# New plan values, the first query block ahead in the head, and the last store on ScalarE's queue

## Chip, cores, metric

One NeuronCore of a Trainium2 chip. The metric is the device time of one execution in microseconds (us); lower is better. Compared are medians and ratios of fast runs. What is read here are the 95% intervals in brackets.

## The reference

Two attention branches over the same `x` (2048 tokens, model width 512, 32 heads of width 16) are mixed by a gate:

```python
def _A_ref(x, wqkv, wo):                     # softmax attention
    q, k, v = ...                            # from x @ wqkv, 32 heads of 16
    p = softmax(einsum("bhqd,bhkd->bhqk", q, k) * 16 ** -0.5)
    return (p @ v, heads joined) @ wo
def _B_ref(x, wqkv, w_phi, wo):              # linear attention with a softmax feature map
    phi_q, phi_k = ...                       # [softmax(q w_phi), softmax(-q w_phi)], same for k
    o = phi_q (phi_k^T v) / (phi_q . sum(phi_k) + 1e-6)
    return (o, heads joined) @ wo
g = sigmoid((x * gate_w).sum(-1))
return g * a + (1 - g) * b
```

(Shortened; the data are bfloat16.) The work that counts is the exponential of 32 x 2048 x 2048 scores.

## The kernel before

Scores are made by PE into a ring of PSUM banks (`ps_ring`, line 934), ScalarE takes the exponential of 1024 columns at a time into `ET` (line 952), and PE multiplies `ET` with V (line 991). 95 key tiles of four heads each go another way, so that ScalarE has less to do: DVE turns their scores into integers (`EW`), GpSimd and DVE work out a polynomial from them, and a DMA of 512 KB adds the two parts up in `ED`; PE then multiplies `ED` with V:

```python
hs = [s.op("pool", ..., lambda e, c=c: e.tensor_scalar(                     # L1079, HS pieces
    self.ED[:, ed.idx, W * c:W * c + W].bitcast(dt.int16), half(1, dt.int16, c, W), 128.0, float(EM), ...
u = s.op("dve", 1.13, lambda e: e.tensor_tensor(self.Em[:], Ef(), Ef(), ALU.mult), ...        # L1084
q = s.op("dve", 0.6, lambda e: e.tensor_scalar(self.Em[:], self.Em[:], E3, E1, ...            # L1086
g_ = s.op("dve", 1.13, lambda e: e.tensor_tensor(Ef().bitcast(dt.int16), Ef(), self.Em[:], ALU.mult), ...  # L1088
v = s.op("pool", SWD[0], lambda e: e.dma_start(                             # L1091
    out().bitcast(dt.int16), Ef().bitcast(dt.int16), accum_op=ALU.add), [g_] + hs, ...)
v.kind = "acc"
...
return s.op("pe", 0.2155, ..., fns=[pv(i) for i in range(4)], deps=vs + [...])   # L1102: waits for the DMA
```

PE's gaps are filled with matmuls by zero (line 1010), most of them 64 rows by 512 columns:

```python
lambda e: e.matmul(self.ps_ot[c:c + nc, :], self.iden[r:r + nr, 0:nc], self.zero[r:r + nr, :], ...)
```

The softmax here doesn't subtract the row's maximum and nothing guards it: scores larger than these inputs give would overflow.

## Time and profile before

| | us |
|---|---|
| time, median of 3 (all) | 823.13 (821.17 to 823.39) |
| first exponential, end of the last | 10.27, 813.00 |
| ScalarE's waits in between | 5.0 in nine pieces of 0.17 or more |
| tail after the last exponential | 7.2 |

From the groups of before, the matmuls that use `ED` (in the last column the idle time just ahead of them, and who ended it):

```profile
L1102 PE MATMUL ps_ot<-ED,Vaug 128*17 128x512 bf16 x380 | 37.3, 383 | 3.7 <-DMA ED<-Ef 3.7
L1102 PEld LDWEIGHTS ps_ot<-ED,Vaug 128*17 128x17 bf16 x380 | 9.2, 87 | 25.4 <-issue 18.0 <-DMA ED<-Ef 7.1
```

The median flight of 4.5 us is under the 4.85 that the plan assumes, so in most cases PE comes to a landed `ED`.

### The profile page before, as it was taken

To read this page: it belongs to the slowest core of one execution; us is meant where nothing else is said; L and a number is where in the kernel's file an instruction comes from. 1 tells how busy PE (TensorE), PEld (TensorE's weight loads), DVE (VectorE), ACT (ScalarE), POOL (GpSimd) and SP (SyncE) were. 2 spreads that over 40 slices of the span, in tenths; PEclk is the share of its full clock that TensorE was granted. 3 is DMA by queue.
4 is the path that set the end of the run, shared out by engine and by line. 5 is a ranking of instruction groups with operands and counts; after the bars stand their busy time and mean duration, and the time that the engine had idled before them with its cause. 6 is when DMAs were issued, how large, how long until landed. Compare 5 with 4: busy or idle time off the path is not lost.

```text
span 820.2 us, 15193 instructions
## 1 busy us (share of the span) xinstructions
PE 766.2 (93%) x6063; PEld 231.3 (28%) x6063; DVE 765.7 (93%) x1140; ACT 801.5 (98%) x906; POOL 396.7 (48%) x451
## 2 busy tenths in 40 slices
PE   8998999999999999999999999889899888989998
PEld 3332333232333333222222222222222222222222
DVE  7999989998689999999999999999999999998993
ACT  6999999899999999999999999999999999999997
POOL 2436435432144555565445654554355555654560
PEclk9999999999999999999999999999999999999999
DMA  6455442444326544446445544543544445424433
GB/s 124 115 100 106 82 97 59 96 95 87 61 54 126 108 90 82 100 94 99 99 93 108 117 96 100 108 94 80 105 78 99 92 97 100 88 56 81 81 71 84
DMA packets 96598, 75.85 MB, mean 92 GB/s; under 512 B 76816, under 2 KB 84368, under 8 KB 96528
## 3 DMA queue, kind: packets, MB, share of 16 engines
q0 software_dynamic: 13680, 49.81, 31.0%
q1 hardware_dynamic: 81504, 24.55, 14.5%
q8 instruction: 48, 0.79, 0.4%
q10 hardware_dynamic: 1344, 0.52, 0.3%
q14 instruction: 22, 0.18, 0.1%
HBM read 3.69 MB, written 2.10 MB: 7 GB/s over the span
## 4 chain that ended last, share of the span: by engine, by line
ACT 70%; DVE 15%; PE 9%; DMA 4%; issue 1%; POOL 1%; ACTq 0%; SPq 0%; POOLq 0%
ACT ET L952 67%; DVE EW L1046 5%; DMA ED<-Ef 4%; PE ps_ring L934 3%; DVE Ef L1088 3%; ACT phi L1250 3%; DVE Em L1084 3%; PE ps_mp L775 2%; DVE Ef L1075 1%; DVE Em L1086 1%; PE ps_ot L991 1%; PE ps_mp L1041 1%; PE ps_mp L856 1%; POOL ED L1079 0%; PE ps_ot L1102 0%
## 5 line engine op out<-in xcount | busy, mean ns | idle before, releaser
L952 ACT ACTIVATE ET<-ps_ring 128x1024 bf16<-128x1024 f32 x834 | 775.2, 1215 | 5.1 <-PE ps_ring L934 4.9
L934 PE MATMUL ps_ring<-qT,kT 64*128 64x512 bf16 x1668 | 325.8, 386 | 38.2 <-ACT ET L952 25.0
L1079 POOL TENSOR_SCALAR ED<-EW 128x512 int16<-128x512 int16 (+1 forms) x266 | 234.4, 907 | 211.3 <-DVE Ef L1088 80.2
L1046 DVE TENSOR_SCALAR EW<-ps_mp 128x512 int32<-128x512 f32 (+1 forms) x306 | 238.4, 811 | 15.5 <-PE ps_mp L1041 14.2
L934 PEld LDWEIGHTS ps_ring<-qT,kT 64*128 64x128 bf16 x1668 | 79.9, 93 | 314.0 <-ACT ET L952 299.7
L991 PE MATMUL ps_ot<-ET,Vaug 128*17 128x512 bf16 x1668 | 148.5, 383 | 0.9 <-DVE T L1131 0.8
L1091 POOL DMA_DIRECT2D ED<-Ef x95 | 86.4, 910 | 109.8 <-DVE Ef L1088 52.3
L1084 DVE TENSOR_TENSOR Em<-Ef 128x2048 f16<-128x2048 f16 x95 | 123.0, 1295 | 0.3
L1075 POOL TENSOR_SCALAR Ef<-EW 128x1024 f16<-128x1024 uint16 (+1 forms) x83 | 79.3, 955 | 86.2 <-DVE EW L1046 20.9
L1088 DVE TENSOR_TENSOR Ef<-Ef,Em 128x2048 int16<-128x2048 f16 x95 | 118.6, 1249 | 0.5
L1041 PE MATMUL ps_mp<-qT,kT 64*128 64x512 bf16 (+1 forms) x380 | 108.4, 380 | 3.0 <-DVE EW L1046 1.2
L1010 PE MATMUL ps_ot<-zero,iden 64*128 64x512 bf16 (+2 forms) x502 | 107.9, 377 | 0.0
L1075 DVE TENSOR_SCALAR Ef<-EW 128x1024 f16<-128x1024 uint16 (+1 forms) x129 | 83.4, 657 | 0.2
L1086 DVE TENSOR_SCALAR Em<-Em 128x2048 f16<-128x2048 f16 x95 | 70.3, 740 | 0.1
L991 PEld LDWEIGHTS ps_ot<-ET,Vaug 128*17 128x17 bf16 x1668 | 33.4, 87 | 77.8 <-issue 69.7
L775 PE MATMUL ps_mp<-Wp,xT 128*128 128x512 bf16 x128 | 42.2, 385 | 0.0
L1250 ACT ACTIVATE phi<-ps_mp 128x512 bf16<-128x512 f32 x64 | 39.7, 757 | 1.9 <-PE ps_mp L775 1.9
L1102 PE MATMUL ps_ot<-ED,Vaug 128*17 128x512 bf16 x380 | 37.3, 383 | 3.7 <-DMA ED<-Ef 3.7
L775 PE MATMUL ps_mp<-xT,WA 128*128 128x512 bf16 (+1 forms) x128 | 39.9, 384 | 0.4 <-ACT xT L760 0.3
L1041 PEld LDWEIGHTS ps_mp<-qT,kT 64*128 64x128 bf16 (+1 forms) x380 | 28.4, 94 | 35.3 <-DVE EW L1046 14.4
L1010 PEld LDWEIGHTS ps_ot<-zero,iden 64*128 64x128 bf16 (+2 forms) x502 | 32.0, 94 | 15.6
L1131 DVE STREAM_TRANSPOSE T<-ps_ot 128x512 f32<-128x512 f32 x31 | 22.0, 709 | 3.9 <-PE ps_ot L991 3.5
(93 smaller groups left out, 411.4 us busy)
## 6 DMA issues: line engine op xcount, KB each, us to landing
ED<-Ef POOLq DMA_DIRECT2D x95, 512.0 KB, 4.5
qT<-qst SPq DMA_DIRECT2D x120, 16.0 KB, 2.0
out_dram<-outt SPq DMA_DIRECT2D x12, 128.0 KB, 1.8
WA<-in_A_wqkv_dram SPq DMA_DIRECT2D x3, 384.0 KB, 4.3
phiT<-phi SPq DMA_TRANSPOSE x48, 3.1
WBV<-in_B_wqkv_dram SPq DMA_DIRECT2D x1, 512.0 KB, 6.8
Wp<-in_A_wo_dram SPq DMA_DIRECT2D x1, 512.0 KB, 6.3
WBV<-in_B_wo_dram SPq DMA_DIRECT2D x1, 512.0 KB, 8.5
```

The costliest lines, as they stand in the source:

```text
L775: m = s.op("pe", self.c_mm(n), lambda e, c=c: e.matmul(self.bk(b)[:, 0:n], lhs(c), rhs(c), start=(c == 0), stop=(c == 3)), deps if c == 0 ...
L934: return lambda e: e.matmul(self.ps_ring[:, x % RING, :], self.kT[r, g // 2, kt * P:(kt + 1) * P], self.qT[r, n % 2, i, :], start=True, st ...
L952: self.o_exp.append(s.op("act", w * 0.434 + 0.039, lambda e, b0=b0, s0=s0, w=w: e.activation(self.ET[:, s0:s0 + w, :], self.ps_ring[:, b0: ...
L991: return lambda e: e.matmul(self.ps_ot[32 * i:32 * i + VSL, :], self.Vaug[:, kt, h, :], self.ET[:, (4 * p + k) % NSLOT, :], start=(kt == 0 ...
L1010: return lambda e: e.matmul(self.ps_ot[c:c + nc, :], self.iden[r:r + nr, 0:nc], self.zero[r:r + nr, :], start=False, stop=False, tile_posi ...
L1041: return lambda e: e.matmul(bank(), self.kT[r, cp, kt * P:(kt + 1) * P], self.qT[r, n % 2, i, :], start=True, stop=True, tile_position=(r. ...
L1046: return s.op("dve", dur, lambda e: e.tensor_scalar(self.EW[:, ew.idx, x * QCH:(x + w) * QCH].rearrange("p (b q) -> p b q", b=w) if w > 1 else
L1075: fs = [s.op("pool", U * 8.26e-4 + 0.28, lambda e, c=c: e.tensor_scalar(self.Ef[:, ef.idx, U * c:U * c + U], half(0, dt.uint16, c, U), flo ...
L1079: hs = [s.op("pool", W * 8.26e-4 + 0.165, lambda e, c=c: e.tensor_scalar(self.ED[:, ed.idx, W * c:W * c + W].bitcast(dt.int16), half(1, dt ...
L1084: u = s.op("dve", 1.13, lambda e: e.tensor_tensor(self.Em[:], Ef(), Ef(), ALU.mult), fs + [self.ed_prev], pr, port=True)
L1088: g_ = s.op("dve", 1.13, lambda e: e.tensor_tensor(Ef().bitcast(dt.int16), Ef(), self.Em[:], ALU.mult), [q], pr, port=True)
L1091: v = s.op("pool", SWD[0], lambda e: e.dma_start(out().bitcast(dt.int16), Ef().bitcast(dt.int16), accum_op=ALU.add), [g_] + hs, pr, frees= ...
```

## The change

Its intent: plan values that were searched again, an earlier first exponential, and an earlier last store. The diff, with values cut:

```diff
-PACE = [1.0638464291072671, 0.45790104673263465]
+PACE = [1.0771457571608845, 0.4579007635970128]
-PIECES = ((2, 2), (2, 4), (4, 4))
+PIECES = ((2, 2), (2, 4), (4, 4), (2, 1), (4, 1))
... LEAD, BOUNDS, RULES, AFF, PAIR, JOINT, OFF, PRI, SHY, FILL, SLIP, POLY, SHAPE: new values
-DVE_COUNT = (..., 3, 4, 4, 2, 4, 2, 3, 4, ...)      # blocks 16 to 23
+DVE_COUNT = (..., 3, 3, 4, 3, 4, 3, 2, 4, ...)      # the sum stays 95
@@ emit_qT
-   [o_ev, self.o_par, self.o_qz[n]], 30 * n - 60 + 2 * x, 12 * n, frees=[st], port=True)
+   [o_ev, self.o_par, self.o_qz[n]], (30 * n - 60 + 2 * x) if n or x > 1 else x - 80, 12 * n, frees=[st], port=True)
@@ store
-   self.stores.append(s.op("sp", 0.06, lambda e: e.dma_start(out2d[t * P:(t + 1) * P, :], src()), [dep],
-        prio, dma=P * D * 2, frees=frees))
+   self.stores.append(s.op("act" if t == NT - 1 else "sp", 0.06, lambda e: e.dma_start(out2d[t * P:(t + 1) * P, :], src()), [dep],
+        1e5 if t == NT - 1 else prio, dma=P * D * 2, frees=frees))
```

A piece whose second number is 1, `(2, 1)` or `(4, 1)`, lets GpSimd write all 2048 columns of `ED` in one instruction.

## The prediction

> **What bounds the kernel now.** I read the page's busy shares first, then its costliest groups, then all the waits of ScalarE, then head and tail in order of time.
>
> ```profile
> PE 766.2 (93%) x6063; PEld 231.3 (28%) x6063; DVE 765.7 (93%) x1140; ACT 801.5 (98%) x906; POOL 396.7 (48%) x451
> L952 ACT ACTIVATE ET<-ps_ring 128x1024 bf16<-128x1024 f32 x834 | 775.2, 1215 | 5.1 <-PE ps_ring L934 4.9
> L1250 ACT ACTIVATE phi<-ps_mp 128x512 bf16<-128x512 f32 x64 | 39.7, 757 | 1.9 <-PE ps_mp L775 1.9
> ```
>
> ScalarE (ACT) is the bound: 98% busy, with 834 exponentials of the softmax scores and 64 of the linear branch. PE and DVE at 93% are near, but PE fills its gaps with matmuls by zero. In the chain that ended last, this runs without a break:
>
> ```profile
> 702.89 108.28 ACT ET L952 x118
> ```
>
> 108.28 / 118 = 0.918 us from one exponential to the next (the 1215 ns of one overlap the next). The chain also has two phi activations in 0.98 us at 106.75. So ScalarE's work is 834 x 0.918 + 32 x 0.98 + 0.14 (two gate activations) = 765.6 + 31.4 + 0.1 = 797.1 us. From 10.27 us, the first exponential, to 813.00, the end of the last, there are 802.7 us. The waits of ScalarE in between:
>
> ```profile
> ACT ET L952 <- PE ps_ring L934: 4.9, 9, 1.9
> ACT phi L1250 <- PE ps_mp L775: 1.9, 1, 1.9
> ```
>
> Of the 4.9 us, 1.87 is the wait for the very first exponential. Left are 3.1 + 1.9 = 5.0 us in nine pieces. 797.1 + 5.0 is 802.1, so the account closes to 0.6 us. Only three things can move the end: when the first exponential starts (10.27), those 5.0 us, and the tail of 820.2 - 813.0 = 7.2 us.
>
> [...]
>
> [...] the flight: 1.7 to 1.8 us for all four last stores.
>
> [...] GpSimd's TENSOR_SCALAR into ED takes 607 to 2115 ns over its forms. At 511.01 a 1024-wide one takes 2.10 us beside DVE work, at 514.35 one takes 1.03.
>
> **The change, part by part.** The plan values feed a scheduler that orders the instructions at build time; I compared the two builds' orders.
>
> *Work.* The number of key tiles given to DVE is 95 in both; one moves from query block 17 to 19 and one from 22 to 21. So ScalarE keeps 834 + 64 activations: change 0. On DVE, conversions into EW go from 74 to 92 double-width and from 232 to 196 single: 18 x 1.218 - 36 x 0.681 = -2.6 us. Ef goes from 105 to 95 wide ones and from 24 to 36 narrow: -10 x 0.708 + 12 x 0.434 = -1.9. Together -4.5 us on an engine beside the bound. On GpSimd, ED becomes 86 of 1024, 136 of 512 and 18 new ones of 2048 (before: 114, 152, none). From 701 and 1181 ns I estimate 2.14 us for one of 2048: -28 x 1.181 - 16 x 0.701 + 18 x 2.14 = -5.8; Ef there adds 12 x 0.616 - 2 x 1.063 = +5.3; net about -0.5. None of this is on the path by itself.
>
> *Head.* Before, the order of time shows:
>
> ```profile
> 8.63 0.35 DVE L796 TENSOR_SCALAR qT<-qst,par 128x512 bf16<-128x512 bf16 x1
> 8.90 0.55 DVE L840 CAST kT<-ps_mp 128x384 bf16<-128x384 f32 x1
> 9.37 0.87 DVE L796 TENSOR_SCALAR qT<-qst,par 128x512 bf16<-128x512 bf16 x3
> 9.50 0.23 PEld L775 LDWEIGHTS ps_mp<-WA,xT 128*128 128x128 bf16 x4 [0.49 <-DVE kT L840]
> 10.27 12.02 ACT L952 ACTIVATE ET<-ps_ring 128x1024 bf16<-128x1024 f32 x13 [1.87 <-PE ps_ring L934]
> ```
>
> The first score pair needs two qT pieces. A kT copy sits between them on DVE, and PE stands four V matmuls, which wait for that copy, ahead of the score. In the new order both qT pieces come first and those four matmuls come after the score. The second qT then starts at about 8.90 instead of 9.37: -0.47 us. The first score moves from 9.84 to about 9.3 to 9.4, the first exponential from 10.27 to about 9.8. The second score still needs the last two qT pieces, which end as before, and PE has two key matmuls ahead of it. It ran at 10.29 and its exponential can start at about 10.73, just as the first one's 0.92 us ends. I take -0.45 us, kept as long as nothing later has a fixed time: ScalarE ran from 10.27 to 69.8 without one wait, so there is room.
>
> *Tail.*
>
> ```profile
> 815.79 1.26 ACT L1386 ACTIVATE outz<-ps_mp,gcol 128x512 bf16<-128x512 f32 x2 [2.80 <-PE ps_mp L1345]
> 816.51 1.88 SPq L1353 DMA_DIRECT2D out_dram<-outz  x4
> 816.95 0.69 ACT L1386 ACTIVATE outz<-ps_ring,gcol 128x512 bf16<-128x512 f32 x1
> 817.94 0.45 SPq L1353 DMA_DIRECT2D out_dram<-outz  x1
> ```
>
> The last evacuation ends at 816.95 + 0.69 = 817.64, but its store is issued at 817.94, behind the third, which went at 817.46. An unqueued one follows its activation by 0.04 (816.51 after 816.47). From ScalarE's own queue it can go at about 817.7: -0.25 us. ScalarE's issues in the head took 0.45 us each, as this one on SP did, so the issue costs nothing more. Evacuations and final matmuls are otherwise in the same order.
>
> *The middle.* The 5.0 us are the rest. The long ones are 0.62 and 0.60 at 69.81 and 73.27 (block 2), 1.94 at 148.29 (block 4), 0.32 at 515.62, 0.60 at 550.24 and 0.20 at 580.00 (blocks 19 to 22). In the two of block 2 and those at 515 and 550, PE stood just before in front of a matmul that waits for an ED transfer, for 0.5 to 0.95 us, with the next scores behind it in its order. The new plan touches those places: other priorities and sharing rules in block 2, other pieces in blocks 4 and 5, and the tile counts of blocks 20 to 22 become 4, 3, 2 from 4, 2, 3. A plan that was chosen again probably removes more of these than it makes. I guess that 5.0 becomes about 3.5: -1.5, the softest term.
>
> Sum: -0.45 - 0.25 - 1.5 = -2.2. From the median of 823.13 that is 820.9 us, a ratio of 0.997.
>
> **Rivals.** First: the head start is given back. If the second score waits for key matmuls that PE now stands ahead of it (their inputs are transposes still landing around 9 to 10 us), ScalarE idles after its first exponential and the gain is 0. [...] Against: before, those matmuls at 10.61 waited only for DVE. The time would be about 821.4.
>
> Second: GpSimd becomes the brake. 18 instructions of about 2.1 us [...]; ED then lands late, PE stands in front of it and the score ring runs dry. For: that is how the waits at 69.81, 73.27 and 550.24 arise, and the last block, with four tiles, now has this shape. Against: GpSimd is 48% busy, [...] and PE's waits for ED are only 3.7 + 7.1 us in all. With a fifth of them losing 1 us each it would cost about 4 us: 825.
>
> Third: the new plan removes nearly all waits of the middle: -4.5 instead of -1.5, and 818.
>
> Fourth: the moved store saves nothing, because ScalarE pays for its issue or for the wait on its own last activation: 0.25 us, too little to see in the total.
>
> **Range and chances.** The hard floor is -0.45 - 0.25 - 5.0 = -5.7 us, or 817.4: even removing every wait is 0.7%, so 2% faster (806.7) is out of reach without less ScalarE work. 2% slower (839.6) needs more than 16 us of new waits, three times all there are. The spread of the runs of before is 821.17 to 823.39, so a median can be off by a microsecond. Eight in ten: 818.3 to 823.9. Faster by over 2%: 0.01; within 2%: 0.98; slower by over 2%: 0.01.
>
> **What would show it.** Right: 834 exponentials at 0.918 us in unbroken stretches, the first at 9.7 to 9.9; the last store on ScalarE's queue within 0.1 us of its activation's end; ScalarE's waits between first and last exponential at 2 to 5 us; the tail about 6.9. Wrong in the head: the first exponential early but a wait of 0.4 us or more before the second or third. Wrong in the middle: waits above 6 us with PE in front of ED matmuls, beside GpSimd's 2048-wide instructions. The whole account is wrong if ScalarE's waits do not explain the difference of the spans to within a microsecond.

(For the exponential the sum used the measured 0.918 us. For the store the page of before gives 1.71 to 1.83 us from issue to landing for the last four, all issued from SP; that the move to ScalarE's queue leaves the flight as it is was not shown. The first rival's order on PE is that of the trace of after, shown with the head below.)

## More of the kernel before

The order of all instructions on each engine is made while the kernel is built, by a list scheduler with estimated durations. It takes an `ED` transfer as landed a fixed time after its issue, `CLEAR[3]`:

```python
CLEAR = [3.0, 1.2, 0.97, 4.85, ...]
if o.kind == "acc":
    o.end = max([o.start + (CLEAR[3] + 0.7 if turns and o.start - turns[-1] < 2.4 else CLEAR[3])] + ...)
```

Each engine is given its instructions in that order, with semaphores for what they wait on.

From the page of before, the `ED` row of the DMA issues (number, size, median us from issue to landing) and the queue that carries packets of the kind "instruction" (packets, MB, share of 16 engines):

```profile
q8 instruction: 48, 0.79, 0.4%
...
ED<-Ef POOLq DMA_DIRECT2D x95, 512.0 KB, 4.5
```

## The result and the profile after

| | before | after |
|---|---|---|
| time, median us (range, runs) | 822.43 (821.17 to 823.39, 6) | 825.62 (822.64 to 826.96, 6) |
| ratio to before, 95% interval | | 1.0037, 1.0016 to 1.0057 |
| first exponential, end of the last (profiled run) | 10.27, 813.00 | 9.24, 813.76 |
| ScalarE's waits in between (all gaps) | 5.2 | 6.8 |
| `ED` landings of 5.2 us or more, of 95 | 8 | 19 |
| longest `ED` flight | 6.7 | 7.7 |

Ratios in this text are the mean time of one kernel's fast runs over the mean of the other's fast runs of the same rounds on the same chip, so not quite the ratio of the medians beside them. The changed kernel is slower by 0.37%, where 0.27% faster was predicted. The profiled run (822.64) is the fastest of the six, so its trace understates the loss.

The page of after, busy shares and the costliest group:

```profile
PE 761.8 (93%) x6038; PEld 229.7 (28%) x6038; DVE 760.7 (93%) x1124; ACT 801.7 (98%) x906; POOL 394.8 (48%) x435
L952 ACT ACTIVATE ET<-ps_ring 128x1024 bf16<-128x1024 f32 x834 | 775.5, 1215 | 6.8 <-PE ps_ring L934 6.4
```

ScalarE does the same work at the same pace (834 exponentials, 1215 ns each). What differs is in its waits, here all that lie between its first and last exponential (us, times, longest):

```profile
ACT ET L952 <- PE ps_ring L934: 6.4, 11, 1.8
ACT phi L1250 <- PE ps_mp L775: 1.3, 1, 1.3
ACT ET L952 <- PE ps_mp L1041: 0.3, 1, 0.3
```

(The first of these also holds 1.3 us before the very first exponential, which do not belong to them.) **The head**, in order of time, after:

```profile
8.81 0.39 PE L934 MATMUL ps_ring<-qT,kT 64*128 64x512 bf16 x2
9.24 1.02 ACT L952 ACTIVATE ET<-ps_ring 128x1024 bf16<-128x1024 f32 x1 [1.33 <-PE ps_ring L934]
9.64 0.59 PE L775 MATMUL ps_mp<-xT,WA 128*128 128x512 bf16 x2 [0.43 <-DMA xT<-in_A_x_dram]
10.16 0.39 PE L934 MATMUL ps_ring<-qT,kT 64*128 64x512 bf16 x2
10.59 1.94 ACT L952 ACTIVATE ET<-ps_ring 128x1024 bf16<-128x1024 f32 x2 [0.32 <-PE ps_ring L934]
```

The first exponential is early, but PE then has two key matmuls ahead of the second score pair, and they wait for a transpose of `x` that lands at 9.6. ScalarE waits 0.32 us for its second piece. **The tail**, after:

```profile
817.72 0.69 ACT L1386 ACTIVATE outz<-ps_ring,gcol 128x512 bf16<-128x512 f32 x1
818.43 0.37 ACTq L1353 DMA_DIRECT2D out_dram<-outz  x1
```

The store now follows its activation at once. From the end of that activation to the end of the span it is 2.43 us; before it was 2.54. **The middle**: the longest wait, after, in order of time from 503 us on:

```profile
504.97 1.44 POOL L1091 DMA_DIRECT2D ED<-Ef  x1 [1.62 <-DVE Ef L1088]
...
511.97 0.39 PE L1102 MATMUL ps_ot<-ED,Vaug 128*17 128x512 bf16 x4 [1.81 <-DMA ED<-Ef]
...
512.73 1.02 ACT L952 ACTIVATE ET<-ps_ring 128x1024 bf16<-128x1024 f32 x1 [1.77 <-PE ps_ring L934]
```

The DMA view of 504 to 512.5 us, after (queue: packets, MB, share; then the one `ED` transfer with its us to landing):

```profile
q8 instruction: 1, 0.02, 1.4%
...
ED<-Ef POOLq DMA_DIRECT2D x1, 512.0 KB, 7.0
```

The transfer took 7.0 us where the plan counts on 4.85. PE stood 1.81 us in front of the matmul that reads it, with the next score pair behind that matmul in its order, and ScalarE ran dry for 1.77 us. An instruction packet started 2.1 us after the issue of this transfer. Several other late transfers had one too, within 3 us of their issue (487.02, 470.28 and 631.06 among them). PE stood for more than 0.1 us ahead of an `ED` matmul at five places after (291.2, 493.2, 512.0, 637.4 and 670.4 us, 4.3 us together), and each of the five transfers had a packet 0.3 to 3 us after its issue. Before there were seven such places, 3.7 us together; three of them (1.7 us) had a packet in that window.

That gave the theories. **T1**: the middle is set by PE standing in front of late `ED` landings. **T1a**: they are late because instruction packets fall into their flight, and the new plan put more of its flights where packets come. **T2**: GpSimd's 2048-wide pieces slow DVE down, and all of `ED` comes late. **T3**: the loss lies in the head.

(What the traces show are instructions that took longer side by side: before, a 1024-wide GpSimd piece took 2.10 us at 511.01 with DVE at work all along, and 1.03 at 514.35 with DVE idle for 0.73 of it; after, the DVE multiplication of line 1088 took 2.12 us at 502.30 beside pieces of GpSimd, with a median of 1.22 over all 95.)

### The profile page after: what moved, and what is told of

Read it like the earlier page. It is cut to its first block, busy times and chain, and to the rows that moved or that the text cites. A ratio compares the mean times of both kernels' runs of the same rounds, so it can differ in the third digit from the quotient of the medians.

```text
span 820.8 us, 15106 instructions
## 1 busy us (share of the span) xinstructions
PE 761.8 (93%) x6038; PEld 229.7 (28%) x6038; DVE 760.7 (93%) x1124; ACT 801.7 (98%) x906; POOL 394.8 (48%) x435
## 4 chain that ended last, share of the span: by engine, by line
ACT 81%; DVE 7%; DMA 5%; PE 4%; POOL 1%; SPq 1%; issue 1%; POOLq 0%
ACT ET L952 77%; DMA ED<-Ef 4%; ACT phi L1250 4%; DVE EW L1046 2%; PE ps_ring L934 1%; DVE Ef L1088 1%; POOL ED L1079 1%; DVE Em L1084 1%; DVE Ef L1075 1%; PE ps_ot L991 1%; DVE Em L1086 1%; DMA phiT<-phi 1%; PE ps_mp L1041 0%; PE ps_mp L775 0%; SPq L693 0%
## 5 line engine op out<-in xcount | busy, mean ns | idle before, releaser
L952 ACT ACTIVATE ET<-ps_ring 128x1024 bf16<-128x1024 f32 x834 | 775.5, 1215 | 6.8 <-PE ps_ring L934 6.4
L1079 POOL TENSOR_SCALAR ED<-EW 128x512 int16<-128x512 int16 (+2 forms) x240 | 219.6, 938 | 195.4 <-DVE Ef L1088 50.0
L1046 DVE TENSOR_SCALAR EW<-ps_mp 128x512 int32<-128x512 f32 (+1 forms) x288 | 238.0, 853 | 20.1 <-PE ps_mp L1041 17.8
L1091 POOL DMA_DIRECT2D ED<-Ef x95 | 88.7, 937 | 126.9 <-DVE Ef L1088 67.1
L991 PE MATMUL ps_ot<-ET,Vaug 128*17 128x512 bf16 x1668 | 146.3, 384 | 0.1
L1075 POOL TENSOR_SCALAR Ef<-EW 128x1024 f16<-128x1024 uint16 (+1 forms) x93 | 88.4, 951 | 87.9 <-DVE EW L1046 29.2
L1088 DVE TENSOR_TENSOR Ef<-Ef,Em 128x2048 int16<-128x2048 f16 x95 | 121.7, 1281 | 0.6
L1084 DVE TENSOR_TENSOR Em<-Ef 128x2048 f16<-128x2048 f16 x95 | 119.9, 1262 | 0.5
L1010 PE MATMUL ps_ot<-zero,iden 64*128 64x512 bf16 (+1 forms) x477 | 110.8, 377 | 0.0
L1041 PE MATMUL ps_mp<-qT,kT 64*128 64x512 bf16 (+1 forms) x380 | 101.8, 382 | 4.2 <-ACT phi L1250 1.2
L1075 DVE TENSOR_SCALAR Ef<-EW 128x1024 f16<-128x1024 uint16 (+1 forms) x131 | 79.5, 619 | 1.0 <-DMA ED<-Ef 0.9
L1010 PEld LDWEIGHTS ps_ot<-zero,iden 64*128 64x128 bf16 (+1 forms) x477 | 32.8, 94 | 15.5
## 6 DMA issues: line engine op xcount, KB each, us to landing
ED<-Ef POOLq DMA_DIRECT2D x95, 512.0 KB, 4.6
WBV<-in_B_wqkv_dram SPq DMA_DIRECT2D x1, 512.0 KB, 7.1
Wp<-in_A_wo_dram SPq DMA_DIRECT2D x1, 512.0 KB, 4.3
WBV<-in_B_wo_dram SPq DMA_DIRECT2D x1, 512.0 KB, 5.1
```

What stands on the lines that cost most here:

```text
L952: self.o_exp.append(s.op("act", w * 0.434 + 0.039, lambda e, b0=b0, s0=s0, w=w: e.activation(self.ET[:, s0:s0 + w, :], self.ps_ring[:, b0: ...
L991: return lambda e: e.matmul(self.ps_ot[32 * i:32 * i + VSL, :], self.Vaug[:, kt, h, :], self.ET[:, (4 * p + k) % NSLOT, :], start=(kt == 0 ...
L1010: return lambda e: e.matmul(self.ps_ot[c:c + nc, :], self.iden[r:r + nr, 0:nc], self.zero[r:r + nr, :], start=False, stop=False, tile_posi ...
L1041: return lambda e: e.matmul(bank(), self.kT[r, cp, kt * P:(kt + 1) * P], self.qT[r, n % 2, i, :], start=True, stop=True, tile_position=(r. ...
L1046: return s.op("dve", dur, lambda e: e.tensor_scalar(self.EW[:, ew.idx, x * QCH:(x + w) * QCH].rearrange("p (b q) -> p b q", b=w) if w > 1 else
L1075: fs = [s.op("pool", U * 8.26e-4 + 0.28, lambda e, c=c: e.tensor_scalar(self.Ef[:, ef.idx, U * c:U * c + U], half(0, dt.uint16, c, U), flo ...
```

## The experiments

The plan is frozen in all of these but the last: the built order is the one named, edited afterwards. All results are correct but for the two kernels that are wrong. "Waits" are ScalarE's between its first and last exponential, in the profiled run.

### Take the wait for ED away

```diff
-                self.ED[:, ed.idx, x * QCH:(x + 1) * QCH].bitcast(dt.bfloat16),
+                self.zero[:],
```

With it goes PE's wait on the transfer, which is now free of a race because nothing reads `ED`; the buffer is freed by the transfer too. Wrong result, same number of everything. For the changed kernel:

> The changed kernel with its plan frozen, where the ED matmuls of PE multiply the zero tile and wait for no ED transfer; the transfers still run (wrong result on purpose). Theory T1 (the middle is set by PE standing in front of late ED landings): ScalarE's waits between first and last exponential fall from 6.8 us to about 1.5 to 3 (the start of block 2, the phi wait at 147 and the second exponential may stay), and the time falls by 3 to 5 us, to about 820 to 822. Rival T2 (GpSimd's 2048-wide pieces slow DVE, which slows the score pairs of its own tiles): the waits stay at 6 us or more and the time stays within 1 us of the changed kernel's.

For the kernel before:

> The same edit on the kernel before. T1: its waits fall from 5.0 us to 2 to 3, the time by 1.5 to 3 us to about 820; with ED out of the way the kernel after is no longer slower than the one before: the two no-wait kernels differ by less than 1 us, the changed one being ahead by the 0.2 of its tail. T2: this one changes by less than 1 us, and the changed kernel without ED waits stays about 3 us behind it.

Measured: changed 818.96 us, 0.9957 of before (0.9943 to 0.9971), waits 4.0. Before 818.33, 0.9953 (0.9940 to 0.9966), waits 2.65. The transfers were as late as ever (19 and 7 at 5.2 us or more). T1 holds: without the wait the 0.37% between the kernels shrinks to 0.04%, which is inside the intervals. The sizes were missed: the waits of the changed kernel stayed above the expected 1.5 to 3 us, and both gains were larger than expected, 6.0 us for the changed kernel against its second run on the same chip (3 to 5) and 4.3 us for before (1.5 to 3). Part of the difference may be the half-clock stretches further below; it was not settled.

### An empty instruction that was none

```diff
+                        ins = engine.nop() if name == "pe" and o.exp is not None and o.exp.grp < NOPS else None
```

> The changed kernel, plan frozen, with one empty instruction ahead of each of PE's first 128 score pairs. This moves the later 16 KB packets of the instruction queue to other times (by about half their spacing of 17 us) and nothing else. T1a (the late landings are ED flights that such a packet hits in its first 2.5 us): the landings at 284.9, 487.0, 505.0, 631.1 and 664.5 come back to 5.1 us or less, others become late, and the 1.77 us wait of ScalarE at 512.7 goes; the time changes by 1 to 3 us either way. Rival (lateness comes [...] from the plan itself): the same ED transfers stay late, the wait at 512.7 stays above 1 us.

This edit put nothing into the program: the trace has the same 6038 weight loads and 151 other instructions on PE's sequencer as that of the changed kernel. The run is the changed kernel a second time: 824.98 us, 1.0034 (1.0017 to 1.0052), and it says nothing on T1a. It does show that 19 landings of 5.2 us or more come again, at the same transfers, and that waits scatter: 9.8 us this time.

### Move the instruction packets

PE gets 6038 weight loads, 6038 matmuls and 151 others by the trace; over 48 packets of 16 KB, which start 10.6 to 21.1 us apart (17.5 in the median of the profile after), that is an estimate of 255 a packet, or 64 bytes each. If the packets bring PE its instructions, adding some early moves all later packets forward. I cut the first half-width fillers in two:

```diff
-            lambda e: e.matmul(ps_ot[...], iden[0:64, 0:128], zero[0:64, :], ...)                  # one of 512 columns
+            lambda e, h=h: e.matmul(ps_ot[0:P, 256*h:256*h+256], iden[0:64, 0:P], zero[0:64, 256*h:256*h+256], ...)  # two of 256
```

64 fillers (128 instructions, half a packet), changed kernel:

> The changed kernel, plan frozen, with the first 64 half-width filler matmuls of PE (all in the first 250 us) given as two of 256 columns each: 128 instructions more for PE to fetch, nearly the same busy time. That should bring the 16 KB instruction packets after 250 us half a spacing (about 8 us) forward. T1a (late landings are ED flights hit by such a packet soon after their issue): the packets behind the ED issued near 285, 487, 505, 631 and 664 us are gone and these land in at most 5.1 us; the waits of 1.8 to 2.1 us of ScalarE near 507 to 513 shrink below 1 us; other ED transfers become late; the time moves by up to 3 us. Rival T2 ([...] the plan's own crowding of transfers): the same ED stay late at 5.9 to 7 us, and so does the wait near 512.

Before:

> The same on the kernel before. T1a with luck (before only happens to have its packets between its ED flights): after 250 us more ED transfers land at 5.2 us or later than the 4 of the 8 that it had there, 8 or more, and it becomes 1 to 3 us slower. T2: still about 4 late after 250 us, time within 0.7 us of before.

32 and 96 fillers (a quarter and three quarters of a packet):

> The changed kernel with only the first 32 half-width fillers halved: 64 instructions more, so the instruction packets of the middle come a quarter of their spacing (about 4 us) earlier. The zero shift gave 1.0037 and 1.0034 of before, the half 1.0004. If the position of the packets sets the difference, this lands anywhere from 1.000 to 1.005, and the number of ED landings at 5.2 us or later with a packet in the first 3 us of their flight follows it. If the plan itself is what costs, a quarter shift gives 1.003 to 1.004 again.

> The same with the kernel before, which had 1.000 at zero and 1.0046 at half. By position: between 0.998 and 1.005. With the four offsets of each kernel there is a mean of each plan over positions: if plan values are neutral once the position is averaged out, the two means differ by less than 0.1 per cent; if the new values cost something by themselves, the changed kernel's mean is 0.2 per cent or more above.

> The changed kernel with the first 96 half-width fillers halved: 192 instructions more, three quarters of the spacing (about 12 us) by about 400 us. By position: 1.000 to 1.005. By plan: 1.003 to 1.004.

> The same with the kernel before. By position: 0.998 to 1.005, and not the same as its half shift; if halving fillers by itself were what cost b_shift its 0.46 per cent, this one, with half as many again, would be at 1.005 or above, and the quarter shift at 1.002 to 1.003.

A whole packet (42 fillers cut into four, one into three), which should bring the packets back to where they were:

> The changed kernel, plan frozen, with the first 42 half-width fillers cut into four and the 43rd into three: 256 instructions more, one whole packet, so that from about 240 us on the packets lie where they lay in the changed kernel itself (only the first 240 us differ). Position theory: ED issued near 285, 453, 487, 505, 631 and 664 us are late again, and the time is back at 1.002 to 1.004 of before, though the quarter, half and three-quarter shifts gave 0.9974, 1.0004 and 0.9966. Rival (cutting fillers up is what helped, for instance by letting PE come sooner to what stands behind them): at 0.997 or below.

> The same with the kernel before. Position theory: back to 1.000 plus or minus 0.0015, though its quarter, half and three-quarter shifts gave 1.0013, 1.0046 and 1.0025. Rival (cutting fillers up costs this kernel time): 1.003 or more.

| instructions added | changed kernel: ratio to before, median | before: ratio, median |
|---|---|---|
| 0 | 1.0037, 825.62; again 1.0034, 824.98 | 1 |
| 64 | 0.9974, 820.49 | 1.0013, 822.44 |
| 128 | 1.0004, 822.02 | 1.0046, 826.13 |
| 192 | 0.9966, 819.02; again 0.9969, 819.54 | 1.0025, 823.54 |
| 256 | 1.0008, 822.77 | 1.0009, 821.83 |

(Intervals are about plus or minus 0.0015 to 0.0025.) The changed kernel's 0.9974 and 0.9966 lie below what I had put down for them by position, 1.000 to 1.005. The packets did move: the one at 507.0 us came at 499.4 with 128 instructions. With 192 the `ED` issued near 504 us no longer has a packet on it, and the DMA view of 503 to 511.5 us of that kernel gives

```profile
ED<-Ef POOLq DMA_DIRECT2D x1, 512.0 KB, 5.2
```

and in order of time from 501 us on

```profile
501.16 12.76 ACT L952 ACTIVATE ET<-ps_ring 128x1024 bf16<-128x1024 f32 x13
...
509.29 0.10 PEld L1102 LDWEIGHTS ps_ot<-ED,Vaug 128*17 128x17 bf16 x4 [0.40 <-DMA ED<-Ef]
```

Thirteen exponentials without a wait, where the changed kernel lost 1.77 + 0.33 us. And the whole packet makes the `ED` issued near 454, 472, 489, 507 and 632 us late again in the changed kernel (18 of 95 at 5.2 us or more) and takes before back to 1.0009. The time of the changed kernel did not come back as expected: 1.0008 (0.9989 to 1.0027) where 1.002 to 1.004 was put on record. So for that kernel the landings follow the packets, but how much of its time does was not pinned down. Cutting fillers does not simply help or hurt: 256 instructions are the most, and neither kernel has its extreme there.

The half packet made the kernel before slower by 0.46%. Of its new waits the two longest, 1.25 us at 383.98 and 0.86 at 525.95, do not stand behind an `ED` matmul. PE stood 1.57 us in front of a score that needs the last of four `qT` transfers, and 1.05 in front of a matmul that needs a transposed `phiT`. Landings by the trace, before against half packet:

```
                          before            half packet (instruction packets at 380.98 and 522.32)
qT, 4th, issued ~377.7    took 4.21 us      took 5.54
ED, issued ~379.6         took 4.41         took 5.59
phiT, issued ~520.3       took 3.04 (517.8) took 4.84
```

For `qT` the other transfers kept their distances, so the packet is what differs. For `phiT` they did not: an `ED` was issued 1.8 us behind it (2.6 before), which may share the blame. So T1a holds in a wider form than I had put it: a packet can delay other transfers in flight too, here a `qT` by 1.33 us, and an `ED` transfer is only the most frequent of those that PE waits for (7 of the 10 waits of a matmul for a transfer in the profile before).

Over the 17 profiles whose PE waits for `ED`, the replanned kernel at the end left out, I sorted the 1615 flights by whether an instruction packet began 0.3 to 3 us after their issue:

```
packet in the flight:  145 flights, median 5.67 us, 78% at 5.2 us or more
none:                 1470 flights, median 4.49 us, 10%
```

So a packet of 16 KB that falls into this window costs a 512 KB transfer 1.2 us in the median. It is not that late transfers merely happen to lie there: 69 transfers of the two plans met a packet in some of these profiles and none in others, and 67 of them took longer with it by their medians (0.9 us in the median in the changed plan, 1.2 in that of before). The DMA records show the delay itself. The `ED` of 504.97 us is moved in 128 pieces of 4 KB. All of them ended by 4.71 us after the issue but for the last six of one chain, which ended at 5.01, 5.31, 5.62, 5.93, 6.24 and 6.55: this chain is 1.8 us behind the others, and the packet was 1.8 us long.

But packets are not the only cause of a late landing. Of the 263 flights of 5.2 us or more only 113 had one in the window (9 of 19 in the profile after, 4 of 8 in that of before), so the larger part has others, which were not tested. (The 22 instruction packets of another queue, q14, 0.18 MB in all, are not counted here.) Of 108 stops of PE of more than 0.1 us ahead of an `ED` that had just landed, 62 us together, those with a packet in the window make up 55, or 36 us.

By its length a packet fits as the cause: the 48 packets took 0.88 to 1.64 us each in the profile before and 0.88 to 1.85 in that of after, about as much as the flights get longer. How a packet and a transfer share the DMA engines was not shown beyond that.

### The same number of cut fillers, late

> The changed kernel, plan frozen, with the last 96 half-width fillers halved (all after about 615 us): as many cut fillers as in the three-quarter shift, but the packets before 615 us stay where the changed kernel has them. Position theory: ED issued near 285, 453, 487 and 505 us land late, the wait near 512 is 1 us or more, time 1.001 to 1.004 of before. Rival (cutting fillers helps by itself): 0.997 like the three-quarter shift.

> The three-quarter shift again, on the same chip as the late cut, since it is the fastest so far. If its 0.9966 was real: 0.9955 to 0.9985 of before, and at least 0.3 per cent ahead of the late cut; waits of ScalarE at 2.5 to 4.5 us. If it was a lucky set of runs: 0.999 or more.

Measured: late cut 822.14 us, 0.9997 (0.9980 to 1.0013); three quarters again 819.54, 0.9969 (0.9950 to 0.9989), on the same chip. The late cut did not come as the position theory had it. Its transfers were late as expected (285, 453, 487, 505 and more, 24 in all) and the wait at 512.8 was there with 1.55 us, yet its time was 0.9997 and not 1.001 to 1.004. (The `ED` of 505.2 us shows that the window of my count is narrow: its packet came 4.7 us after the issue, just ahead of the last piece of the transfer, 4 bytes that ended at 5.65 with everything else done by 4.73.) The difference of the two cuts, 0.28%, just misses the 0.3% I had asked for. So the best offset is real and repeats, but part of the way from 1.0035 to it, up to 0.35%, may come from something that goes with cutting fillers, or from the chip.

### The half-clock stretches

The traces record the clock granted to TensorE. Between the two ends of a run it is 1.0, with stretches of 0.5 that are 3.413 us long; one, in the kernel before with half a packet, is of double length. In the second run of the changed kernel, busy time by engine in the two stretches around 514.76 us (length; PE, PEld, DVE, ACT, POOL; PEclk, DMA share, GB/s):

```profile
511.35:514.76 3.41, 1.66 (x16) 0.42 (x14) 3.41 (x4) 2.76 (x4) 3.21 (x4) 1.00 0.84 120
514.76:518.18 3.42, 3.42 (x13) 0.62 (x9) 2.21 (x3) 2.05 (x2) 1.13 (x2) 0.50 0.00 0
```

and its exponentials from 513 us on:

```profile
515.41 1.02 ACT L952 ACTIVATE ET<-ps_ring 128x1024 bf16<-128x1024 f32 x1 [1.30 <-PE ps_ring L934]
516.92 1.02 ACT L952 ACTIVATE ET<-ps_ring 128x1024 bf16<-128x1024 f32 x1 [0.49 <-PE ps_ring L934]
518.63 2.85 ACT L952 ACTIVATE ET<-ps_ring 128x1024 bf16<-128x1024 f32 x3 [0.69 <-PE ps_ring L934]
```

This is the same place as the 1.77 us wait in the first run. PE stood in front of the same late `ED`, was busy for 1.66 of 3.41 us, and its next 3.41 us ran at half clock, so that scores came too slowly for ScalarE: 2.48 us lost instead of 1.77. In the kernel before with half a packet, 381.6 to 388.5 us shows the same behind the late `qT`:

```profile
381.60:385.04 3.44, 1.63 (x15) 0.32 (x15) 1.43 (x3) 2.19 (x4) 2.78 (x3) 1.00 0.60 117
385.04:388.45 3.41, 3.41 (x22) 0.47 (x22) 3.29 (x5) 2.73 (x3) 1.38 (x2) 0.50 0.61 118
```

The records show steps of one length: every stretch is 3.413 us long or twice that, full clock began anywhere from 4.48 to 10.34 us into the span, and from there the times at full clock are multiples of 3.413 too: 812.37 us (238.0 times) in the profile before, 61.44 and 750.93 (18.0 and 220.0 times) in that of after. Whether a stop of PE costs a stretch was not the same in two runs of one program: the first run of the changed kernel had no such stretch near 512 us, the second had one. I took it that this depends on how the stop lies to the steps. But this is not shown, and the lie of the steps can't be all. In the late cut, counted in steps of 3.413 us from its own half-clock stretch at the end, PE was busy for less of one step than above and kept full clock in the next:

```profile
509.65:513.06 3.41, 1.49 (x12) 0.40 (x9) 3.41 (x5) 1.86 (x3) 2.07 (x2) 1.00 0.51 39
513.06:516.47 3.41, 3.37 (x25) 0.84 (x23) 2.28 (x3) 3.41 (x4) 1.86 (x2) 1.00 0.00 0
```

So PE's busy time in the trace alone does not tell when the clock is halved: a stretch followed 1.66 us busy of 3.41 and 1.63 of 3.44, and none followed 1.49 of 3.41. What starts a stretch stays open.

The mean clock of a run counts the stretches: each takes 1.71 us of full clock out of 820. A straight-line fit over the 143 fast runs of 17 kernels, with a constant of its own for each kernel, gives 0.98 us (standard error 0.10) for each stretch. Before had 1.3 of them in a run on average, the changed kernel 1.7. At equal numbers the changed kernel is still 2.3 us behind by the spans of the core, so by this fit stretches are not the main term. Stretches and stops of PE come together, so the fit can't tell what each of the two costs by itself.

### GpSimd's wide pieces

```diff
-  one tensor_scalar of 2048 columns into ED
+  two of 1024, one after the other (18 places)
```

> The changed kernel, plan frozen, each of the 18 GpSimd ED instructions of 2048 columns emitted as two of 1024. T2 (the long GpSimd instructions [...] delay the issue of ED): fewer issues above 1.1 us, fewer late landings, waits of ScalarE down from about 7 to 10 us to 5, time 2 to 3 us lower, level with before. T1a: late landings and time as in the changed kernel, within 0.7 us.

Measured: 823.47 us, 1.0015 (0.9995 to 1.0035), which overlaps with the 1.0037 of the changed kernel and with before. But what T2 said of the trace did not come: 20 landings of 5.2 us or more (19 before the edit), nine issues above 1.1 us (nine), waits 6.0. T2 has no support; a share of it of 2 us or less can't be ruled out by the time alone.

### Head and tail

The two key matmuls of the changed kernel put behind the second score pair:

> The changed kernel, plan frozen, the two key matmuls that PE had between the first and the second score pair put behind the second. If the head's gain was given back by that order (my first rival): the wait of 0.32 to 0.60 us before the second exponential at 10.6 falls to below 0.15 and the time by 0.2 to 0.5 us, unless the third score then waits for the same transfer. If it is swallowed further on at the first ED wait near 70 us, the wait there grows by the same amount, and the time stays.

The head's reordering alone, on the order of before:

> The kernel before, plan frozen, with the head's reordering done by hand: both qT pieces of the first score pair ahead of the kT copy on DVE, the first score pair ahead of the four V matmuls on PE. My prediction gave this part 0.45 us. If it holds: the first exponential comes 0.45 us sooner after the qst cast (2.37 us before, about 1.9 here), no wait before the second above 0.15, and 0.9995 of before or a bit less. If PE or DVE makes the second pair wait: a wait of 0.3 us or more before the second exponential and 1.000.

The store alone:

> The kernel before with the last output store alone issued from ScalarE's queue; all other orders identical. The last activation's end to the end of the span goes from 2.56 us to about 2.3 to 2.4; the time falls by 0.2 us, which five rounds hardly tell from 0. Rival (ScalarE's issue costs as much as the queue did): 2.5 us or more remain, time unchanged.

Measured: 825.93 us, 1.0035 (1.0012 to 1.0057); 822.16 us, 0.9998 (0.9979 to 1.0018); 821.32 us, 0.9985 (0.9971 to 0.9998). The times can't resolve these parts (the third interval leaves out 1, but its 1.2 us are far more than the change in the tail below, and nothing on record explains them), but the traces can, since the head is the same in every kernel of a plan. From the start of the cast into `qst` to the first exponential it is 2.36 to 2.37 us in all seven profiles with the order of before, 1.83 in nine of the ten with the changed one (2.65 in the tenth, whose PE ran slowly), and 1.84 in the reordered before. The gain of 0.54 us does not always last, as the head of the reordered before shows:

```profile
9.53 2.01 ACT L952 ACTIVATE ET<-ps_ring 128x1024 bf16<-128x1024 f32 x2 [1.33 <-PE ps_ring L934]
...
11.81 1.02 ACT L952 ACTIVATE ET<-ps_ring 128x1024 bf16<-128x1024 f32 x1 [0.27 <-PE ps_ring L934]
```

By the thirteenth exponential, six of the nine profiles had kept about 0.43 us (one of them 0.36), and three, in which the second pair waited, 0.17 or less, one of these being behind; the mean is 0.29. So the head is no loss on average, and T3 is out. The swap took the wait before the second exponential away (under 0.1 us) but in its profile the whole head was late: PE ran slowly until about 10 us. The first eight projection matmuls of that head,

```profile
6.44 2.31 PE L775 MATMUL ps_mp<-xT,WA 128*128 128x512 bf16 x8 [0.26 <-ACT xT L760]
```

and of the changed kernel's first run,

```profile
6.34 1.26 PE L775 MATMUL ps_mp<-xT,WA 128*128 128x512 bf16 x8 [0.29 <-ACT xT L760]
```

differ by 1 us at the same work. So this run is no clean test of the swap. The first exponential lies between 8.94 and 11.05 us over the profiles, a scatter of 2.1 us where the whole change was predicted to bring 2.2, so one profile's head can't be set against another's by the clock; only distances within a head can. The 1.03 us between the first exponentials in the table of the result are 0.54 of order and 0.49 of a head that was late as a whole before: full clock began at 7.49 us there and at 5.89 after, which fits.

From the last activation's end to the end of the span it is 2.53 to 2.55 us in the seven profiles with the order of before and the store on SP, and 2.43 to 2.45 in twelve with the store on ScalarE, this one among them: the tail is worth 0.10 us.

### A plan with room for late landings

```diff
-CLEAR = [3.0, 1.2, 0.97, 4.85, ...
+CLEAR = [3.0, 1.2, 0.97, 6.0, ...
```

> The changed kernel planned again with an ED landing assumed at 6.0 us after its issue, not 4.85, so that PE comes to the ED matmuls about 1.1 us later and a landing of up to 6 us no longer stops it. If the late landings alone cost the time: waits of ScalarE at 2 to 4 us, and 0.995 to 0.999 of before. Rival (room for a late landing is paid for with score pairs that come late elsewhere, since every choice of the plan values was fitted to 4.85): 1.002 or more, with waits that do not stand behind ED matmuls.

Measured: 846.10 us, 1.0285 (1.0264 to 1.0306), waits 22 us in 22 pieces, the tail 12.9 us. PE stood in front of `ED` for only 1.9 us (3.7 before), so that part worked. But everything was planned anew with values that were fitted to 4.85, and score pairs came late elsewhere. The rival was right.

## Why the prediction was wrong

**The account.** It closes after as before: 9.24 for the first exponential, 6.8 of waits, 797.1 of work, 7.1 of tail make 820.2, and the span is 820.8. Only start, waits and tail could move the end; that step was right.

**Head, -0.45.** Measured: -0.54 at the first exponential, kept at -0.43 or lost, -0.29 on average. The mechanism was right, and the first rival (key matmuls with a late transpose ahead of the second pair), which I had put aside because those matmuls "waited only for DVE" before, holds in some of the heads.

**Tail, -0.25.** Measured: -0.10. The store is issued 0.28 us earlier behind its activation, but it lands 1.99 us after its issue on ScalarE's queue and not 1.83 as on SP's, and from its issue the span lasts 2.41 us and not 2.24. The step that gave the whole earlier issue to the end was too large by 0.15.

**Middle, -1.5.** This step failed: "A plan that was chosen again probably removes more of these than it makes." The waits went from 5.2 to 6.8 us in the fastest run and to 9.8 in another, where 5.0 to 3.5 was predicted. I had seen that they arise where PE stands in front of an `ED` transfer, but I took the flight of a transfer for a property of the plan's own work. It depends on instruction packets as well, which are in no plan: 11 of 95 flights had one in their first 3 us after the change and 6 before, and such a flight is 1.2 us longer in the median. PE's stops ahead of `ED` with a packet in this window went from 1.7 us before to 4.3 and 4.9 in the two profiles of the changed kernel, those without one from 1.9 to 0 and 1.6. So what was added lies at the stops with a packet. The comparison at equal offsets shows how much of this is luck. Over the offsets 0, 64, 128 and 192 the changed kernel's mean ratio is 0.9995 ((1.00355 + 0.9974 + 1.0004 + 0.99675) / 4) and that of before 1.0021 ((1 + 1.0013 + 1.0046 + 1.0025) / 4). Over these four the new plan is 0.26%, or 2.1 us, the better one; at the one offset it was built with it is the worse one by 0.35%. With single offsets up to 0.7% apart, four of them do not show that it is better in general. I had not expected this order: I had allowed the means to be equal or the changed one above.

**Second rival (GpSimd as the brake, 825).** Its number came true, its cause did not: `ED` did land late and the score ring did run dry, but splitting the wide pieces (1.95 us each in the trace, 2.14 by the estimate) left the late landings as they were. (The 3.7 + 7.1 us that the prediction held against this rival are the records of matmuls and weight loads at partly the same stops, so they are no sum.)

**What stays open.** At the packets' original place the changed kernel ran at 1.0037 and 1.0034, the whole-packet shift at 1.0008 and the late cut at 0.9997. Fewer half-clock stretches (0.6 against 1.7 in a run) account by the fit for about 1 us of the 2.8 us (by the spans of the core) between the late cut and the changed kernel. The rest was not settled; other chips, the early part of the program and the cut fillers themselves are not told apart. That the new plan is better on average rests on four offsets, reached by cutting fillers. What makes the late landings without a packet was not tested.

**A version that beats both.** The changed kernel with 96 fillers halved: 819.02 and 819.54 us, 0.9966 and 0.9969 of before, and correct. It is tuned to one place of the packets: with 128 and 256 instructions added in place of 192 the same kernel was at 1.0004 and 1.0008, so an edit that changes PE's instruction count can lose the gain.

## What to carry to other kernels

When the bound engine's work stands behind a DMA in another engine's order (here PE stood 1.81 us in front of one `ED` transfer and ScalarE lost 1.77), the scatter of that DMA is in your critical path: look at the longest flights (7.7 us here) and not at the median (4.6). A difference of a few tenths of a per cent between two instruction orders may come from the place of the instruction packets; shift both kernels by a quarter, half and three quarters of a packet before calling one of them better. And when the bound engine is 98% busy, the same stop of PE need not cost the same twice: near 512 us ScalarE lost 1.77 us without a half-clock stretch behind it and 2.48 with one.
